# Turning batch 1's last x pair, q rest and x rest by transfer instead of on TensorE, with a new order of steps around tile 1's first products

## The chip, the cores and the metric

The kernel runs on one core of one Trainium2 chip. The metric is the device time of one execution in microseconds (us); lower is better. One execution is also recorded by the hardware profiler, and all views below come from that record.

## The reference

A linear attention over 8 batches, 8 heads, 576 tokens and a head size of 64 feeds a mixture of four dense two-layer experts, whose outputs are added with normalised weights:

```python
phi = lambda x: np.where(x > 0, x, np.exp(x) - 1.0) + 1.0
q_p, k_p = phi(q), phi(k)
kv  = einsum('bhsd,bhse->bhde', k_p, v);  z = k_p.sum(axis=2)
x   = einsum('bhsd,bhde->bhse', q_p, kv) / (einsum('bhsd,bhd->bhs', q_p, z) + 1e-6)
x   = x.transpose(0, 2, 1, 3).reshape(4608, 512)
p   = domain_probs / (domain_probs.sum(-1) + 1e-9)
out = sum over e of p[:, e] * (relu(x @ w1[e]) @ w2[e])      # 4 experts, 512 -> 1024 -> 512
```

## The kernel before

**Tiles and batches.** The 4608 rows are nine tiles of 512. Tiles 0 to 7 hold the first 512 tokens of one batch each; the last 64 tokens of every batch, its rest, are gathered in one more tile, `xT_left`, which is computed last but one. While TensorE multiplies tile j, the attention of batch j+1 is done beside it. `First` is batch 0, whose attention opens the kernel; `Batch` is every other one.

**Attention of one batch.** The raw k, v and q arrive in four pieces each (steps `load`, into a ring of six buffers, tag `raw`), the rests in `rl` (`load_left`). `k0` to `k3` and `q0` to `q3` compute phi on ScalarE, `km` and `qm` finish it on VectorE, `v0` to `v3` cast v on ScalarE into `vp`, `lk`, `lv`, `lq` do the same for the rests. `kv` multiplies k and v. q must be turned (features on the partitions) before the numerators `nd`, and their result x must be turned again into `xT` before the tile's products. A turn is done in one of two ways: four 128x128 products with an identity on TensorE and a copy out of PSUM on ScalarE (`pe_qT`, `pe_xT`, `pe_qTl`, `pe_xl`), or a transposing DMA issued on SyncE's queue (`dma_qT`, `dma_xT`, `dma_qTl`, and the end of `nd_left`). Batch 1 turns q on TensorE, three of its four x pairs by DMA, and pair 2 (`b1.xT2`), its q rest (`b1.qTl`) and its x rest (`b1.xl`) on TensorE. Batches 2 to 7 turn everything by DMA.

**Tile products.** Tile 0 of experts 1 to 3 and all later tiles use seven half-size products for layer 1, in blocks. Block d of expert e and tile j has the steps `p1.jed` to `p7.jed` and `c22.jed`. `p1` multiplies into PSUM bank b, and ScalarE copies b to bank e; `p2` adds into e and ScalarE takes the relu; `p6` adds into b and ScalarE copies it out (`u2`); `p5` starts e anew; `p7` adds into b and ScalarE copies it out (`u3`); `c22` (VectorE) takes the relu of e plus `u3`; `p4` adds into b, relu on ScalarE; `p3` adds into e, and VectorE takes the relu with `u2`. `p1` reads x pairs 0 and 1, `p2` reads pairs 2 and 3. The token sums `ts1.0` to `ts1.3` (GpSimd) feed p5, p6, p7 and p4; `ts1.1` needs pairs 2 and 3. Layer 2 of tile 0 is made of quarters: `y3.21` is expert 3, row group 2, quarter 1, two products of 512 columns; the last quarter is followed by an addition into `acc` (VectorE) and, for expert 3, by a store. Later tiles use the products `m` and the sums `hs` (GpSimd).

**Order.** Nothing is scheduled by a machine here. Every step has a name; a step that yields is resumed each time its name comes up again. The strings of `EARLY` in `CFG` list the names in the order in which the steps are emitted up to the start of tile 2, and positions in `CFG` sort the rest; every engine and every DMA queue runs its instructions in that order. All of `load`, `load_left` and the transposing DMAs of batches 1 and up stand in SyncE's one queue (but for a few loads of batch 1 on GpSimd's), and a DMA that waits there holds up all behind it.

The line that picks pair 2 in `batch_steps`, and the one that leaves batch 1 out in `nd_left`:

```python
put(at["xt"][i], f"b{b}.xT{i}", bt.pe_xT if i == 2 else bt.dma_xT, i)
for u in range(2) if self.b != 1 else ():
```

Of the kernel before, what the change touches and what calls it, by code (L numbers as in the profile page):

```python
# [12 lines left out]
FP16 = mybir.dt.float16  # L13
# [17 lines left out]
            v=(18.1, 19.16, 22.55, 30.55),  # L31
            k=(-5.5, 26.3, 27.5, 28.5),
# [5 lines left out]
            q=(36.4, 36.95, 40.2, 43.4),  # L38
            qd=(37.75, 39.0, 40.55, 44.7),
            lq=54.05,  # L40
            lqd=54.5,
            qt=(42.1, 45.0, 45.8, 46.25),
            nd=(46.7, 47.0, 47.05, 47.8),
            xt=(48.15, 50.45, 51.45, 54.8),
            qtl=57.23,
            nl=71.0,
            xl=95.55,
# [13 lines left out]
            lqd=38.3,  # L61
# [74 lines left out]
    ),  # L136
# [4 lines left out]
def kernel(  # L141
# [86 lines left out]
    def aps(shape, dtype, name, more=""):  # L228
        return ppm.tile(shape, dtype, tag=CFG["BANK"].get(now[0] + more, "s"), bufs=2, name=name)
# [67 lines left out]
    class Batch:  # L297
# [132 lines left out]
                    in_=self.ql[us].rearrange("p h d -> p (h d)"),  # L430
                )

        def pe_qTl(self):
            ps = aps([P, 2, P], FP16, "psum_ql")
            for a in range(2):
                nc.tensor.transpose(out=ps[:, a], in_=self.ql[:, 2 * a : 2 * a + 2], identity=identh)
            yield
            for u in range(2):
                us = slice(u * HP, (u + 1) * HP)
                nc.scalar.copy(out=self.qTl[:, :, u, us], in_=ps[:, :, us])  # L440

        def pe_xl(self):
            ps = aps([P, 2, P], FP16, "psum_xl")
            for a in range(2):
                nc.tensor.transpose(out=ps[:, a], in_=self.xl[:, a], identity=identh)
            yield
            c0 = self.b * SL
            for u in range(2):
                us = slice(u * HP, (u + 1) * HP)
                nc.scalar.copy(out=xT_left[:, 2 * u : 2 * u + 2, c0 : c0 + SL], in_=ps[:, :, us])  # L450

        def pe_qT(self, pair, eng=nc.vector):
            ps = aps([P, CM, P], FP16, "psum_qT")
            g, a = divmod(pair, 2)
# [59 lines left out]
        def nd_left(self, side_by_side=False):  # L514
            ps = aps([P, 3, 2, DE], FP32, "psum_nl")
            for a in range(2):
                for u in range(2):
                    us = slice(u * HP, (u + 1) * HP) if side_by_side else slice(0, P)
                    nc.tensor.matmul(  # L519
                        out=ps[us, a],  # L520
                        lhsT=self.qTl[:, a, u, us],
                        rhs=self.kvz[:, 2 * u + a],
                        start=side_by_side or u == 0,
                        stop=side_by_side or u == 1,
                        skip_group_check=side_by_side,
                    )
            yield
            self.xl = pa.tile([P, 2, P], FP16, tag="xsl", bufs=1, name="x_sl")
            self.norm(self.xl, ps, 2)
            yield  # L530
            for u in range(2) if self.b != 1 else ():
                us = slice(u * HP, (u + 1) * HP)
                c0 = self.b * SL
                nc.sync.dma_start_transpose(
                    out=xT_left[:, 2 * u : 2 * u + 2, c0 : c0 + SL],
                    in_=self.xl[us].rearrange("p a i -> p (a i)"),
                )

        def pe_xT(self, pair):
            ps = aps([P, CM, P], FP16, "psum_xT")  # L540
            for c in range(CM):
                nc.tensor.transpose(out=ps[:, c], in_=self.x[:, pair, c], identity=identh)
            yield
            if self.xT is None:
                self.new_xT()
            nc.scalar.copy(
                out=self.xT[:, pair],
                in_=ps.rearrange("p c i -> p (c i)"),
            )

        def dma_xT(self, pair):
            if self.xT is None:
# [410 lines left out]
    def batch_steps(bt, nxt, put, at, at_next):  # L963
# [34 lines left out]
            put(at["l" + n], f"b{b}.l{n}", bt.left_act, n)  # L998
            put(at["l" + n + "d"], f"b{b}.l{n}m", bt.left_dve, n)
        put(at["kv"], f"b{b}.kv", bt.kv)  # L1000
        put(at["lqd"] + 1, f"b{b}.next", load_left, "k", "v")
        put(at["lqd"] + 1.001, f"b{b}.nextq", load_left, "q")
        if not first:
            put(at["lqd"] + 2, f"b{b}.qTl", bt.dma_qTl)
        if first:
            put(at["qtl"], f"b{b}.qTl", bt.pe_qTl)
            for i in range(NPAIR):
                put(at["qt"][i], f"b{b}.qT{i}", bt.pe_qT, i, nc.scalar)
                for hf in range(2):
                    put(at["nd"][i], f"b{b}.nd{i}{hf}", bt.nd, i * CM + 2 * hf, 2)  # L1010
                put(at["xt"][i], f"b{b}.xT{i}", bt.pe_xT if i == 2 else bt.dma_xT, i)
            for i in range(NRAW):
                put(at["next"][i], f"b{b}.load{i}", load, len(mine) + i)
        else:
            for g in range(2):
                put(at["qT"][g], f"b{b}.qT{g}", bt.dma_qT, g)
            for i in range(6):
                put(at["nd"][i], f"b{b}.nd{i}", numerators, 3 * i, min(3, NPAIR * CM - 3 * i))
        if nxt is None or b in (1, 4):
            put(at["nl"] - 4.9 * (b == 4), f"b{b}.nl", bt.nd_left)  # L1020
        else:
            put(2 * NSLOT * E + at_next["kv"] - 1e-6, f"b{b}.nl", bt.nd_left, True)
        if first:
            put(at["xl"], f"b{b}.xl", bt.pe_xl)

    def warm(n):

# [9 lines left out]
    with tc.manual_schedule(  # L1037
# [76 lines left out]
        for j in range(0, NTILES - 1):  # L1114
            at = base + 2 * NSLOT * E * (j - 1) if j else 0.0

            def put(pos, *g, at=at):
                put_at(at + pos, *g)
# [65 lines left out]
```

## Time and profile before

| | |
|---|---|
| time, median of 3 runs | 483.89 us (483.45 to 484.4) |
| the profiled execution, its own time | 483.89 us |
| its span, first to last instruction | 482.1 us |
| TensorE (PE) busy | 476.2 us, 99% |
| VectorE (DVE) busy | 379.1 us, 79% |
| GpSimd (POOL) busy | 358.8 us, 74% |
| ScalarE (ACT) busy | 329.9 us, 68% |
| mean DMA rate | 112 GB/s, 54.06 MB |
| granted TensorE clock | 0.999 |

The 1.8 us between the span and the time lie outside the recorded instructions. In the views, `L897` is line 897 of the kernel before, `PE` is TensorE's products, `SPq` SyncE's DMA queue; a timeline row is start, duration, engine, line, operation, and how many instructions were merged. A PE row's duration is that of overlapping instructions, so the spacing of the starts tells what a group costs. A row of DMA issues ends with the us from issue to landing.

### The profile page before, as it was taken

The page shows a single profiled execution, that of the slowest core. Times are in us where ns is not written, and L with a number is a line of the kernel's source. Part 1 is how long each engine was busy: PE and PEld are TensorE (multiplying, and loading weights), DVE is VectorE, ACT ScalarE, POOL GpSimd, SP SyncE. Part 2 cuts the span into 40 slices and gives each one's busy share as a digit, 9 for nine tenths or more (in the row PEclk, how much of TensorE's full clock was granted, in tenths as well). Part 3 has the DMA queues.
Part 4 walks back from the last instruction along what each step waited for, and adds up shares of the span by engine and source line. Part 5 has one row for each costly group of instructions (what it writes and reads, how often), then busy time and mean ns, then how long its engine had stood idle before and what let it go on. Part 6 is the DMA issues. An engine that isn't in the chain of part 4 may idle for free.

```text
span 482.1 us, 12029 instructions
## 1 busy us (share of the span) xinstructions
PE 476.2 (99%) x4565; PEld 406.7 (84%) x4565; DVE 379.1 (79%) x794; ACT 329.9 (68%) x659; POOL 358.8 (74%) x343
## 2 busy tenths in 40 slices
PE   9999999999999999999999999999999999999996
PEld 3776757898889888988888888988898888888886
DVE  5868998897868796888678885988787756775677
ACT  4688969956795599649884888478954465446540
POOL 5666144788966986789777977697769877987775
PEclk9999999999999999999999999999999999999999
DMA  8999997532454154624562347323320020003002
GB/s 291 218 217 262 234 224 225 141 91 82 132 158 107 31 158 148 135 57 116 171 151 51 104 130 182 68 68 113 93 44 13 1 88 1 1 2 88 2 1 87
DMA packets 80489, 54.06 MB, mean 112 GB/s; under 512 B 45536, under 2 KB 73184, under 8 KB 80432
## 3 DMA queue, kind: packets, MB, share of 16 engines
q1 hardware_dynamic: 70288, 40.89, 31.9%
q0 software_dynamic: 8896, 11.34, 12.1%
q10 hardware_dynamic: 1248, 1.08, 0.7%
q8 instruction: 35, 0.57, 0.5%
q14 instruction: 22, 0.18, 0.1%
HBM read 45.16 MB, written 9.44 MB: 113 GB/s over the span
## 4 chain that ended last, share of the span: by engine, by line
PE 93%; DMA 2%; POOL 2%; DVE 1%; ACT 1%; issue 1%; SPq 0%; POOLq 0%
PE py L840 38%; PE pb L897 25%; PE pe L897 19%; PE py L745 6%; PE ph L685 1%; PE psum_nd L500 1%; DMA rawq<-in_q_dram 1%; DMA xT<-x_sb 1%; PE psum_kv L472 1%; PE pb L840 1%; POOL tt L878 1%; PE pe L840 1%; POOL hs L813 0%; POOL hs L807 0%; PE psum_nl L519 0%
## 5 line engine op out<-in xcount | busy, mean ns | idle before, releaser
L736 DVE SCALAR_TENSOR_TENSOR acc<-py,p_sb,acc 128x256 f32<-128x256 f32 (+1 forms) x382 | 182.2, 488 | 44.4 <-PE py L840 39.8
L881 DVE CUSTOM_DVE_ANT_0 h<-pe,u 128x512 f16<-128x512 f32 x140 | 96.1, 688 | 43.1 <-PE pe L897 26.1
L897 PEld LDWEIGHTS <-w 128*128 128x128 f16 x1120 | 108.7, 98 | 16.3
L807 POOL TENSOR_TENSOR hs<-h 128x512 f16<-128x512 f16 x64 | 73.8, 1154 | 55.6 <-DVE h L881 54.2
L840 PEld LDWEIGHTS <-h 128*128 128x128 f16 x1024 | 99.7, 98 | 11.6
L840 PE MATMUL py<-w,h 128*128 128x256 f16 x744 | 106.6, 273 | 0.0
L908 ACT COPY u<-pb 128x512 f32<-128x512 f32 x140 | 82.7, 593 | 31.0 <-PE pb L897 28.7
L809 POOL TENSOR_TENSOR hs<-hs,h 128x512 f16<-128x512 f16 x64 | 74.2, 1160 | 24.3 <-PE py L840 21.8
L897 PEld LDWEIGHTS <-s 128*128 128x128 f16 x840 | 81.2, 98 | 11.8
L897 PE MATMUL pb<-tt,w 128*128 128x256 f16 x560 | 83.9, 273 | 0.0
L840 PEld LDWEIGHTS <-hs 128*128 128x128 f16 x768 | 74.2, 98 | 9.2 <-POOL hs L807 0.3
L813 POOL TENSOR_TENSOR hs<-h,hs 128x512 f16<-128x512 f16 x64 | 74.8, 1168 | 1.2 <-POOL h L811 0.6
L840 PE MATMUL py<-t,hs 128*128 128x256 f16 x496 | 74.3, 273 | 0.1
L811 POOL TENSOR_TENSOR h<-h 128x512 f16<-128x512 f16 x64 | 74.3, 1161 | 0.1
L930 ACT ACTIVATE h<-pe 128x512 f16<-128x512 f32 x70 | 42.1, 601 | 41.7 <-PE pe L897 41.2
L923 ACT COPY pe<-pb 128x512 f32<-128x512 f32 x70 | 40.1, 574 | 40.1 <-PE pb L897 14.8
L951 ACT ACTIVATE h<-pb 128x512 f16<-128x512 f32 x70 | 41.9, 600 | 5.4 <-PE pb L897 5.4
L897 PE MATMUL pb<-tt,s 128*128 128x256 f16 x280 | 41.9, 273 | 0.0
L897 PE MATMUL pe<-tt,s 128*128 128x256 f16 x280 | 41.9, 273 | 0.0
L897 PE MATMUL pe<-xT,s 128*128 128x256 f16 x248 | 37.1, 273 | 0.0
L897 PE MATMUL pe<-xT,w 128*128 128x256 f16 x248 | 37.1, 273 | 0.0
L897 PE MATMUL pb<-xT,w 128*128 128x256 f16 x248 | 36.9, 273 | 0.0
(134 smaller groups left out, 596.9 us busy)
## 6 DMA issues: line engine op xcount, KB each, us to landing
w<-in_moe_w_dram POOLq DMA_DIRECT2D x14, 512.0 KB, 10.3
out_dram<-acc SPq DMA_DIRECT2D x28, 256.0 KB, 2.5
rawb<-in_k_dram SPq DMA_DIRECT2D x24, 256.0 KB, 3.2
rawb<-in_q_dram SPq DMA_DIRECT2D x24, 256.0 KB, 2.7
rawb<-in_v_dram SPq DMA_DIRECT2D x24, 256.0 KB, 3.0
out_dram<-acc SPq DMA_DIRECT2D x12, 128.0 KB, 2.3
w<-in_moe_w_dram POOLq DMA_DIRECT2D x4, 256.0 KB, 5.5
rawb<-in_k_dram POOLq DMA_DIRECT2D x4, 256.0 KB, 10.4
```

Of the source, the lines that this page charges most:

```text
L736: nc.vector.scalar_tensor_tensor(out=acc, in0=ps, scalar=pscal, in1=acc, op0=AO.mult, op1=AO.add)
L807: nc.gpsimd.tensor_tensor(out=hs[0], in0=a21, in1=a22, op=AO.add)
L809: nc.gpsimd.tensor_tensor(out=hs[1], in0=hs[0], in1=a11, op=AO.subtract)
L811: nc.gpsimd.tensor_tensor(out=a21, in0=a11, in1=a21, op=AO.subtract)
L813: nc.gpsimd.tensor_tensor(out=hs[3], in0=a12, in1=hs[1], op=AO.subtract)
L840: nc.tensor.matmul(out=ps, lhsT=lhsT(k), rhs=rhs[:, k], start=first and k == 0, stop=k == FH - 1, skip_group_check=True,)
L881: nc.vector._custom_dve(TENSOR_ADD_SAT, out=out, in0=ps, in1=u, s0=BIG, s1=0.0)
L897: nc.tensor.matmul(out=ps[:, kk], lhsT=lk(kc), rhs=rhs[:, kc], start=first and kk == 0 and kc == 0, stop=kc == 1, skip_group_check=True,)
L908: nc.scalar.copy(u, self.b)
L923: nc.scalar.copy(self.e5, self.b)
L930: nc.scalar.activation(self.h[:, :, 0, 0:NH], self.e5, AF.Relu)
L951: nc.scalar.activation(self.h[:, :, 1, 0:NH], self.b, AF.Relu)
```

## The change

The three turns of batch 1 that TensorE did go by transposing DMA; `pe_qTl`, `pe_xl` and `pe_xT` go. One step `next` that loaded the rests of k and v becomes `nextk` and `nextv`. The steps between batch 1's numerators and the first `m` products of tile 1 stand in a new order; from `b2.qm0` on the names follow as before.

```diff
-            for u in range(2) if self.b != 1 else ():
+            for u in range(2):
                 us = slice(u * HP, (u + 1) * HP)
                 c0 = self.b * SL
                 nc.sync.dma_start_transpose(
                     out=xT_left[:, 2 * u : 2 * u + 2, c0 : c0 + SL],
...
-        put(at["lqd"] + 1, f"b{b}.next", load_left, "k", "v")
-        put(at["lqd"] + 1.001, f"b{b}.nextq", load_left, "q")
-        if not first:
-            put(at["lqd"] + 2, f"b{b}.qTl", bt.dma_qTl)
+        for n in range(3):
+            put(at["lqd"] + 1 + n / 1000, f"b{b}.next" + "kvq"[n], load_left, "kvq"[n])
+        put(at["qtl"] if first else at["lqd"] + 2, f"b{b}.qTl", bt.dma_qTl)
         if first:
-            put(at["qtl"], f"b{b}.qTl", bt.pe_qTl)
...
-                put(at["xt"][i], f"b{b}.xT{i}", bt.pe_xT if i == 2 else bt.dma_xT, i)
+                put(at["xt"][i], f"b{b}.xT{i}", bt.dma_xT, i)
...
-        if first:
-            put(at["xl"], f"b{b}.xl", bt.pe_xl)
```

The order, from the third x pair on, before:

```
... b1.xT3 b1.next
b2.load2 b2.load1 b1.load4 b1.load3 b1.load2 y2.03 b1.qT2 p4.031 y2.20 y2.21 b1.qT2 b1.lq p4.030 b2.k1 y2.22 b1.load5 b1.nextq b2.load0 y2.03 b1.lqm
p3.031 b1.nd21 y2.23 y2.30 b1.nd20 y2.31 y2.32 t1.3 y2.23 b1.nd20 b1.nd21 y2.33 y2.10 b1.xT2 y2.11 y2.12 y2.13 y2.33 p3.030 y3.20 p3.031 b2.km1 p1.101
p1.100 y3.21 y3.22 y3.23 y3.30 b1.xT2 b2.k0 b2.lk p1.101 p1.100 p2.101 ts1.0 ts1.1 ts1.2 b2.ones ts1.3 b2.load4 y3.31 p6.100 p2.101 p6.100 p2.100
p2.100 b2.v3 y3.32 y3.33 p7.100 p5.101 p5.100 p7.100 b2.k2 p6.101 y3.00 y3.01 p4.100 p6.101 b2.k3 p4.100 b2.lv y3.02 p7.101 y2.13 b2.km0 t2.0 t2.1
...
```

And after:

```
... b1.xT3 b1.nextk
y2.03 b1.qT2 p4.031 y2.20 y2.21 b1.qT2 b1.lq p4.030 b2.k1 y2.22 y2.03 b1.lqm p3.031 b1.nd21 y2.23 y2.30 p3.030 b1.nd21 y2.23 y2.31 b1.nd20 y2.32
b1.nd20 y2.33 y2.10 b1.xT2 b2.load2 b2.load1 b1.load4 b1.load3 b1.load2 b1.load5 b1.nextv b1.nextq b2.load0 y2.11 y2.12 y2.33 b2.k0 y3.20 y2.13 p3.031
t1.3 ts1.0 y3.21 ts1.1 p1.100 y3.22 p1.100 ts1.2 p1.101 y3.23 p2.100 ts1.3 b2.load4 p1.101 b2.lk p2.101 p6.100 y3.30 p6.101 p2.100 p6.100 p5.100
p7.100 b2.km0 y2.13 p6.101 b2.v0 p7.100 pr1 y3.23 y3.00 y3.01 b2.km1 t3.0 t2.0 y3.02 p7.101 p4.100 b1.qTl b2.load3 b2.k2 p7.101 p2.101 p4.100 b2.v3
b2.load5 y3.23 b2.load10 b2.lv b2.v2 b2.k3 c22.100 p3.100 y3.31 ...
```

`b1.load2` fetches batch 2's v0, `b2.load2` its q0, `b2.load1` its v3, `b1.load4` v1, `b1.load3` k2 and `b1.load5` k3. `b1.nl`, which ended with the TensorE turn `b1.xl`, now ends with two transposing DMAs; they come up after the last name of `EARLY`, ahead of batch 3's four q loads.

More of the change, by code (lines that the diff above doesn't have):

```diff
@@ L431, in dma_qTl @@
                 )
[L433 to L450, printed above, removed]
         def pe_qT(self, pair, eng=nc.vector):
@@ L537, in nd_left @@
                 )
[L539 to L549, printed above, removed]
         def dma_xT(self, pair):
```

34 rows, old and new, of the table nl are left out of this document.

## Prediction

> **What bounds the kernel now.** I read the page first, then who waits for whom on PE, then PE's timeline at the three places the change touches.
>
> ```profile
> PE 476.2 (99%) x4565; PEld 406.7 (84%) x4565; DVE 379.1 (79%) x794; ACT 329.9 (68%) x659; POOL 358.8 (74%) x343
> PE warm_ps L1030 <- DVE qz L194: 1.2, 1, 1.2
> PE psum_num L658 <- DVE kvz L647: 0.6, 1, 0.6
> PE psum_num L658 <- ACT kvz L647: 0.4, 1, 0.4
> ```
>
> TensorE is busy all the time, and its three listed waits belong to the opening of batch 0 (warm-up products and `x_norm`). From there on the time is the sum of TensorE's products. Work taken from TensorE is worth its own length, work taken from others nothing, unless something new comes too late for TensorE. So the prediction has two terms: what TensorE saves, and which hand-overs become late in the new order.
>
> **What TensorE saves.** A group's cost is the spacing of starts in the timeline, since the durations overlap.
>
> ```profile
> 64.33 1.89 PE L745 MATMUL py<-w,h 128*128 128x512 f16 x8
> 66.06 0.39 PE L542 MATMUL psum_xT<-identh,x_sb 128*128 128x128 f16 x4
> 66.28 1.89 PE L745 MATMUL py<-w,h 128*128 128x512 f16 x8
> L445 PE MATMUL psum_xl<-identh,x_sl 128*128 128x128 f16 x2 | 0.3, 220 | 0.0
> 123.43 0.60 PE L897 MATMUL pb<-tt,w 128*128 128x256 f16 x4
> 123.86 0.84 PE L840 MATMUL py<-t,hs 128*128 128x256 f16 x4
> 124.54 0.60 PE L897 MATMUL pb<-tt,s 128*128 128x256 f16 x4
> ```
>
> The four products of `b1.xT2` take 66.28 - 66.06 = 0.22 us, 0.055 each. `b1.xl` has two of the same form (the L445 row), `b1.qTl` two more: eight in all, 8 x 0.055 = 0.44 us. That is the whole certain gain. One other hole is near: the group at 123.86 takes 0.68 us where its neighbour takes 0.43, so TensorE stands 0.25 us. The change touches nothing that I can tie to it, so I keep it; if it went, the gain would be 0.69. ScalarE's five copies go too, worth nothing by themselves.
>
> **Where the new order is tight: `b1.xT2`.** From 66.06 both programs have done the same on TensorE. From the rows above a quarter of layer 2 (two products of 512 columns) costs 1.73 / 4 = 0.43 us, four products of 256 columns also 0.43; I use 0.435 for a step. In the new order nine steps (y2.11, y2.12, y3.20, y2.13, y3.21, p1.100, y3.22, p1.101, y3.23) lie before p2.100, the first reader of pair 2: it is wanted at 66.06 + 9 x 0.435 = 69.97.
>
> ```profile
> 65.47 0.42 DVE L488 TENSOR_TENSOR x_sb<-psum_nd,recip 128x256 f16<-128x256 f32 x1
> 65.34 1.27 SPq L318 DMA_DIRECT2D rl<-in_v_dram  x2
> xT<-x_sb SPq DMA_TRANSPOSE x27, 2.4
> xT<-x_sb SPq DMA_TRANSPOSE x1, 5.3
> xT<-x_sb SPq DMA_TRANSPOSE x1, 8.1
> q0 software_dynamic: 818, 0.81, 122.5%
> 66.00:67.00 1.00, 1.00 (x10) 0.58 (x8) 1.00 (x2) 0.52 (x2) 0.82 (x1) 1.00 0.59 131
> 68.66 1.15 POOL L878 TENSOR_TENSOR tt<-xT 128x512 f16<-128x512 f16 x1
> ```
>
> Pair 2 is whole on VectorE at 65.47 + 0.42 = 65.9 now. In the new order one relu (p3.030) goes ahead of it and one weight difference (t1.3) goes behind it; I take these as equal. SyncE's queue is free from 65.34, because the two loads of v's rest that started there move behind. So the transfer is issued at 65.9. The median of 27 landed 2.4 us after issue: 68.3, which leaves 1.65 us. Two earlier ones of this stage took 8.1 and 5.3, while GpSimd's weight loads kept the DMA engines full (the software queue's row is from 56 to 60). By 66 that queue is empty and the DMA share is 0.59 (last but one row), so I take 2.4, and keep 8.1 as the far end. The Trainium skill, "DMA: Bandwidth & Descriptors", section "Queues, rings and completion order", has each DMA engine alternate between the queues that have work for it, packet by packet. By that rule 2.4 holds here and 8.1 doesn't, since no software transfer is moved; the trace agrees as far as the shares go. GpSimd's sums behind the transfer, 1.15 each, would be ready at 69.5 (ts1.1; p6.100 wants it at 70.85) and 70.6 (ts1.2; p7.100 wants it at 72.59). No loss here.
>
> **Where it is late: batch 2's v0.** The transfer stands in SyncE's queue ahead of six raw loads, and it waits there for VectorE; they wait with it.
>
> ```profile
> 66.71 0.55 SPq L340 DMA_DIRECT2D rawb<-in_q_dram  x1
> 68.89 0.42 SPq L340 DMA_DIRECT2D rawb<-in_v_dram  x1
> 132.35 2.45 SPq L534 DMA_TRANSPOSE xT_left<-x_sl  x2
> rawb<-in_q_dram SPq DMA_DIRECT2D x1, 256.0 KB, 3.0
> rawb<-in_v_dram SPq DMA_DIRECT2D x1, 256.0 KB, 4.4
> rawb<-in_k_dram SPq DMA_DIRECT2D x1, 256.0 KB, 5.6
> ```
>
> A transposing DMA holds the queue 2.45 / 2 = 1.2 us, so the first raw load goes out at 65.9 + 1.2 + 0.1 = 67.2 instead of 66.71, and v0, the fifth, at 68.89 + 0.5 = 69.4. It took 4.4 us to land (five 256 KB loads go out within 2.2 us and share the engines); the first of the six took 3.0, the last 5.6. I take its own 4.4: 73.8. Ends: 72.4 and 75.0.
>
> When does ScalarE want it? The old order cast v3 first, long after v0 was issued; the new one casts v0 first.
>
> ```profile
> 68.01 0.84 ACT L399 ACTIVATE kz<-rl 64x256 f16<-64x256 f32 x2
> 68.88 0.39 ACT L401 ACTIVATE psum_el<-rl 128x256 f32<-128x256 f32 x1
> 69.20 1.03 ACT L923 COPY pe<-pb 128x512 f32<-128x512 f32 x2
> 70.61 0.60 PE L897 MATMUL pe<-xT,w 128*128 128x256 f16 x4
> 71.30 0.60 ACT L930 ACTIVATE h<-pe 128x512 f16<-128x512 f32 x1 [1.07 <-PE pe L897]
> 72.11 0.59 ACT L908 COPY u<-pb 128x512 f32<-128x512 f32 x1 [0.21 <-PE pb L897]
> 72.61 0.60 ACT L930 ACTIVATE h<-pe 128x512 f16<-128x512 f32 x1
> 78.16 1.69 ACT L381 CAST vp<-rawb 128x512 f16<-128x512 f32 x3
> L881 DVE CUSTOM_DVE_ANT_0 h<-pe,u 128x512 f16<-128x512 f32 x140 | 96.1, 688 | 43.1 <-PE pe L897 26.1
> ```
>
> ScalarE starts 0.69 us after the group that it waits for (71.30 against 70.61). p1.101 begins on TensorE at 66.06 + 7 x 0.435 = 69.10, so its copy begins at 69.79. Behind it stand, by the spacing of these rows: the copy 0.48, the k rest 0.87, its exponential 0.32, the relu of p2.100 0.50, the copies `u2` of p6.100 and p6.101 0.50 each. ScalarE is at v0 at 72.95. It waits there 73.8 - 72.95 = 0.85 us. A cast takes (1.69 - 0.63) / 2 = 0.53, so the copy `u3` of p7.100, queued behind it, runs from 74.4 and takes 0.59: ready at 75.0.
>
> Two readers want `u3`. p4.100 overwrites what `u3` copies; it is the 21st step after 66.06, wanted at 66.06 + 20 x 0.435 = 74.76, and so comes 0.2 late. c22.100 on VectorE reads `u3`, 0.69 long: ready at 75.7; p3.100, which TensorE reaches at 75.0 + 0.435 = 75.4, waits 0.3 more for it. Together 0.5 us of standing. Before it p7.100 wants the `u2` copy of p6.100 (71.95 + 0.59 = 72.54) at 72.59, an edge that costs 0 to 0.1; I count it within the 0.5. Behind it VectorE has slack again, since TensorE is late by the same 0.5. If v0 lands at the early end, 72.4, ScalarE doesn't wait and nothing is lost; at the late end, 75.0, ScalarE waits 2.05 and TensorE stands 0.5 + 1.2 = 1.7.
>
> **Covered parts.** The rows that do it:
>
> ```profile
> 114.44 0.37 SPq L340 DMA_DIRECT2D rawb<-in_k_dram  x1
> 117.27 8.82 SPq L340 DMA_DIRECT2D rawb<-in_q_dram  x4
> 84.76 0.42 SPq L717 DMA_DIRECT2D out_dram<-acc  x1
> out_dram<-acc SPq DMA_DIRECT2D x28, 256.0 KB, 2.5
> 87.89 0.50 ACT L734 ACTIVATE acc<-py,p_sb 128x256 f32<-128x256 f32 x1
> ```
>
> The x rest's two transfers fall into SyncE's idle time between 114.44 + 0.37 = 114.8 and 117.27; they need 2.45 us and fill it. Without that cover the four q loads behind them would slip by as much, of the 8.8 us they spend waiting for buffers anyway. Nobody reads the result before the last but one tile. The q rest's two transfers hold up two q loads and four stores by 2.45 us. The store that frees the fourth `acc` buffer goes out just ahead of the last one in the new order, about 84.7 by that one's row, and lands at 84.7 + 2.5 = 87.2, before ScalarE's addition at 87.89: 0.7 us of slack, which each further us of lateness would eat and then cost ScalarE.
>
> **The sum.** The profiled execution took 483.89 us, which is the median too, so no correction is needed. 483.89 - 0.44 + 0.5 = 483.95 us.
>
> **The rivals.**
>
> *v0 in time.* Its load lands within 3.55 us (69.4 to 72.95). For it: the first load took 3.0, and the two rest loads that were ahead are gone. Against it: the transposing DMA has taken their place, and v0 has four raw loads ahead. Only the gain is left: 483.89 - 0.44 = 483.45; with the hole at 123.86 gone too, 483.2. Chance 0.22.
>
> *v0 very late.* It lands like k3, 5.6 us after issue: 483.89 - 0.44 + 1.7 = 485.15. Slower. It decides from a landing about 5.2 us after issue. Chance 0.14.
>
> *Pair 2 late.* The transfer lands more than 69.97 - 65.9 = 4.1 us after issue; from then every us is a us of TensorE, while v0's wait melts away behind it. At 5.3 us: 483.89 - 0.44 + 1.2 = 484.65; at 8.1: 483.89 - 0.44 + 4.0 = 487.45. It is slower by what can be told from 5.5 us on. Against it stands the empty software queue. Chance 0.08.
>
> *Turns dearer than they look.* If a turn held TensorE for more than its spacing, eight of them would bring more. The starts give no room: 66.28 follows 66.06 by 0.22 and the next products run at full pace, so at the 220 ns that the L445 row gives for one instruction it would be 8 x 0.22 = 1.8 us, 482.1 without other losses. The Trainium skill, "TensorE: Matmul & The Clock Gate", section "Part 4: PE-mode transpose", gives about 275 ns for one such turn within a kernel, which would make it 2.2 us, an estimate from that page; the trace's 55 ns contradicts it as a cost. Chance 0.05.
>
> **How the numbers follow.** About 0.2% (1 us) is what a measurement of this kernel can tell from no change. My forecast, 483.95, has 0.51, with 483.6 to 484.4 around it. Within 0.2% (482.9 to 484.9) lie the forecast, v0 in time, and a little of the late cases: 0.51 + 0.22 + 0.04 = 0.77. Slower by more: most of v0 very late (0.13) and most of pair 2 late (0.05): 0.18. Faster by more: only dearer turns, 0.05. The range from 483.2 to 485.0 leaves out the far part of the two late cases and the dear turns.
>
> **What would show it.** In the profile after: no rows of the identity products outside batch 0 and `b1.qT`; an xT transfer issued near 65.9 and landing near 68.3; v0's load issued near 69.4; ScalarE idle before its first cast, released by a DMA, near 73; and PE starts with a hole of 0.2 to 0.5 us near 75, before the groups of p4.100 and p3.100. A PE without holes from 66 to 90 makes v0 in time the right case; a hole just before p2.100 makes pair 2 the culprit; holes after 90 that were not there before would mean that I missed a hand-over.

## The result and the profile after

| | before | after |
|---|---|---|
| median of 6 runs | 483.86 us (483.35 to 484.47) | 486.12 us (485.81 to 487.49) |
| profiled execution | 483.89 us | 485.82 us |
| its span | 482.1 us | 484.0 us |
| granted TensorE clock | 0.999 | 1.000 |

The ratio is 1.0049, 95% interval 1.0034 to 1.0063: slower by some 2.3 us, outside the predicted range (483.2 to 485.0), where no difference was the likeliest. In the kernel after, other line numbers stand for the same code: L866 is the products `p`, L714 tile 0's layer 2, L809 the products `m`, L877 the copies `u2` and `u3`, L703 ScalarE's addition into `acc`, L686 the store, L523 the transfer of an x pair.

The first part of the page (busy us, share, instructions):

```profile
PE 476.6 (98%) x4557; PEld 406.1 (84%) x4557; DVE 379.1 (78%) x794; ACT 329.0 (68%) x654; POOL 359.0 (74%) x343
```

Who waits for whom on PE (us in total, times, the longest):

```profile
PE py L809 <- ACT acc L703: 0.9, 2, 0.5
PE pb L866 <- ACT u L877: 0.6, 1, 0.6
```

TensorE has eight products fewer, as meant, and two kinds of waits that the kernel before didn't list. The first place is the predicted one. ScalarE's timeline of the kernel after (start, us, engine, line, and in brackets the idle time before with its releaser):

```profile
71.92 1.07 ACT L877 COPY u<-pb 128x512 f32<-128x512 f32 x2
74.35 0.62 ACT L381 CAST vp<-rawb 128x512 f16<-128x512 f32 x1 [1.36 <-DMA rawb<-in_v_dram]
74.88 0.58 ACT L877 COPY u<-pb 128x512 f32<-128x512 f32 x1
```

PE's timeline there:

```profile
74.30 0.60 PE L866 MATMUL pb<-tt,w 128*128 128x256 f16 x4
75.51 0.61 PE L866 MATMUL pb<-tt,w 128*128 128x256 f16 x4 [0.62 <-ACT u L877]
76.23 0.60 PE L866 MATMUL pe<-xT,s 128*128 128x256 f16 x4
```

SyncE's queue in the timeline:

```profile
65.86 1.24 SPq L523 DMA_TRANSPOSE xT<-x_sb  x1
67.14 0.58 SPq L340 DMA_DIRECT2D rawb<-in_q_dram  x1
67.83 0.90 SPq L340 DMA_DIRECT2D rawb<-in_v_dram  x2
68.83 0.43 SPq L340 DMA_DIRECT2D rawb<-in_k_dram  x1
69.35 0.42 SPq L340 DMA_DIRECT2D rawb<-in_v_dram  x1
```

The DMA issues of narrow windows, with us from issue to landing (pair 2's transfer, v0):

```profile
xT<-x_sb SPq DMA_TRANSPOSE x1, 3.0
rawb<-in_v_dram SPq DMA_DIRECT2D x1, 256.0 KB, 4.8
```

v0's load went out at 69.35 and landed 4.8 later. ScalarE stood 1.36 us before its cast, the copy `u3` behind it began at 74.88, and TensorE stood before p4.100 and p3.100: 75.51 - 74.30 - 0.435 = 0.77 and 76.23 - 75.51 - 0.435 = 0.28.

The second place wasn't in the sum. ScalarE's timeline of the kernel after:

```profile
89.84 0.47 ACT L703 ACTIVATE acc<-py,p_sb 128x256 f32<-128x256 f32 x1 [0.94 <-DMA out_dram<-acc]
```

SyncE's queue:

```profile
85.02 0.37 SPq L340 DMA_DIRECT2D rawb<-in_v_dram  x1
85.48 0.89 SPq L686 DMA_DIRECT2D out_dram<-acc  x2
```

PE's timeline:

```profile
89.78 1.19 PE L809 MATMUL py<-w,hs 128*128 128x256 f16 x8
90.80 0.60 PE L866 MATMUL pe<-xT,s 128*128 128x256 f16 x4
91.77 0.60 PE L809 MATMUL py<-w,h 128*128 128x256 f16 x4 [0.37 <-ACT acc L703]
```

The landing of the store issued at 85.48:

```profile
out_dram<-acc SPq DMA_DIRECT2D x1, 256.0 KB, 4.3
```

What SyncE's queue waited for from 78 to 87 us (us in total, times, the longest):

```profile
SPq L340 <- ACT psum_ee L371: 2.1, 3, 1.4
```

ScalarE needs an `acc` buffer at 89.84 - 0.94 = 88.90; the store that frees it went out at 85.48, right behind a load of batch 3, and landed at 89.8. That load (85.02) had itself stood in the queue, 1.4 us, for a raw buffer that ScalarE had still to read. TensorE stood 91.77 - 90.80 - 0.435 = 0.53, and 0.15 (1.02 less eight products' 0.87) just before. The third place is late, PE's timeline again:

```profile
242.49 0.60 PE L866 MATMUL pb<-xT,w 128*128 128x256 f16 x4
243.58 0.60 PE L809 MATMUL py<-w,h 128*128 128x256 f16 x4 [0.49 <-ACT acc L703]
```

That is 0.65 us. The hole of 0.25 that the kernel before had at 123.86 isn't there. With three short holes near 72.6, 78.0 and 92.5, 0.18 together, the account closes: -0.44 - 0.25 + 1.05 + 0.68 + 0.65 + 0.18 = +1.87, against 485.82 - 483.89 = 1.93 in the profiled executions.

### The profile page after: what moved, and what is told of

Same layout as the page of the kernel before. It is cut to its first block, busy times and chain, and to the rows that moved or that the text cites. A ratio compares the mean times of both kernels' runs of the same rounds, so it can differ in the third digit from the quotient of the medians.

```text
span 484.0 us, 12015 instructions
## 1 busy us (share of the span) xinstructions
PE 476.6 (98%) x4557; PEld 406.1 (84%) x4557; DVE 379.1 (78%) x794; ACT 329.0 (68%) x654; POOL 359.0 (74%) x343
## 4 chain that ended last, share of the span: by engine, by line
PE 91%; DVE 3%; DMA 3%; ACT 1%; issue 0%; SPq 0%; ACTq 0%; DVEq 0%
PE py L809 38%; PE pb L866 24%; PE pe L866 18%; PE py L714 4%; PE ph L654 1%; PE psum_nd L481 1%; DMA rawq<-in_q_dram 1%; DMA rawb<-in_v_dram 1%; DMA out_dram<-acc 1%; PE psum_kv L453 1%; PE pb L809 1%; DVE h L850 1%; PE pe L809 1%; DVE acc L705 0%; PE psum_nl L500 0%; DVE kpos L565 0%
## 5 line engine op out<-in xcount | busy, mean ns | idle before, releaser
L866 PEld LDWEIGHTS <-w 128*128 128x128 f16 x1120 | 108.7, 98 | 17.8 <-ACT u L877 1.1
L809 PEld LDWEIGHTS <-h 128*128 128x128 f16 x1024 | 99.7, 98 | 12.9 <-issue 1.2
L809 PE MATMUL py<-w,h 128*128 128x256 f16 x744 | 106.4, 273 | 0.9 <-ACT acc L703 0.9
L877 ACT COPY u<-pb 128x512 f32<-128x512 f32 x140 | 82.6, 592 | 29.9 <-PE pb L866 27.7
L866 PEld LDWEIGHTS <-s 128*128 128x128 f16 x840 | 81.1, 98 | 11.9 <-issue 0.3
L866 PE MATMUL pb<-tt,w 128*128 128x256 f16 x560 | 83.9, 273 | 0.6 <-ACT u L877 0.6
L809 PEld LDWEIGHTS <-hs 128*128 128x128 f16 x768 | 74.2, 98 | 8.9 <-issue 0.3
L809 PE MATMUL py<-t,hs 128*128 128x256 f16 x496 | 74.1, 273 | 0.0
L866 PE MATMUL pe<-tt,s 128*128 128x256 f16 x280 | 42.0, 273 | 0.0
L866 PE MATMUL pb<-tt,s 128*128 128x256 f16 x280 | 41.9, 273 | 0.0
L866 PE MATMUL pe<-xT,s 128*128 128x256 f16 x248 | 37.1, 273 | 0.1
L866 PE MATMUL pb<-xT,w 128*128 128x256 f16 x248 | 37.1, 273 | 0.0
L809 PE MATMUL py<-w,hs 128*128 128x256 f16 x248 | 37.0, 273 | 0.0
```

The costliest lines, as they stand in the source:

```text
L809: nc.tensor.matmul(out=ps, lhsT=lhsT(k), rhs=rhs[:, k], start=first and k == 0, stop=k == FH - 1, skip_group_check=True,)
L866: nc.tensor.matmul(out=ps[:, kk], lhsT=lk(kc), rhs=rhs[:, kc], start=first and kk == 0 and kc == 0, stop=kc == 1, skip_group_check=True,)
L877: nc.scalar.copy(u, self.b)
```

## The experiments

All ratios are to the kernel before, in five rounds on the same chip for the kernels of one job; the kernel before had medians of 484.01 (E1 to E4), 483.65 (E5 to E8) and 484.12 us (E10 to E13; the numbers go by the runs' names). The opening of batch 0 differs by up to about 0.6 us between executions of any of these kernels, so differences below that are read from the holes, not from one execution's time.

| | edit | median, us | ratio, 95% interval |
|---|---|---|---|
| E1 | after, v0's load first of the six | 484.77 | 1.0013 (1.0004 to 1.0023) |
| E2 | after, the store ahead of batch 3's loads | 485.17 | 1.0031 (1.0019 to 1.0043) |
| E3 | both | 483.71 | 1.0002 (0.9993 to 1.0010) |
| E4 | old order, turns by transfer | 484.21 | 1.0002 (0.9993 to 1.0011) |
| E5 | new order, turns on TensorE | 485.12 | 1.0037 (1.0024 to 1.0050) |
| E6 | before, one turn eight times | 485.00 | 1.0026 (1.0016 to 1.0035) |
| E7 | after, two later loads moved by position | 485.52 | 1.0041 (1.0027 to 1.0056) |
| E8 | E3, the same move | 483.77 | 1.0004 (0.9995 to 1.0012) |
| E10 | after, pair 2 alone on TensorE | 484.60 | 1.0011 (1.0001 to 1.0021) |
| E11 | E3, the two loads behind `qT0` | 483.85 | 0.9993 (0.9981 to 1.0005) |
| E12 | before, the two loads behind `qT0` | 484.28 | 1.0006 (0.9997 to 1.0015) |
| E13 | E4, the two loads behind `qT0` | 484.01 | 1.0001 (0.9988 to 1.0013) |

**E1: v0's load first.** Theory: the place of v0's load in SyncE's queue makes the first holes.

```diff
-b1.xT2 b2.load2 b2.load1 b1.load4 b1.load3 b1.load2 b1.load5
+b1.xT2 b1.load2 b2.load1 b1.load4 b1.load3 b2.load2 b1.load5
```

> The changed kernel with one edit: in SyncE's queue the load of batch 2's v0 takes the place of q0's, first of the six instead of fifth. Theory (late v0): the holes near 74.3 and 75.5 us (0.77 and 0.28) go, since v0 would land near 71 and ScalarE wants it at 73.0; the hole near 91 stays, because the store of y3.0 still stands behind the batch 3 loads: 486.1 - 1.05 = 485.1 us. Rival (the transfers themselves crowd queue and DMA engines, whatever is loaded first): some other load or the turn becomes late, 486 us.

ScalarE's timeline of E1:

```profile
72.58 0.65 ACT L381 CAST vp<-rawb 128x512 f16<-128x512 f32 x1
...
89.03 0.47 ACT L703 ACTIVATE acc<-py,p_sb 128x256 f32<-128x256 f32 x1 [1.12 <-DMA out_dram<-acc]
```

Who waits on PE:

```profile
PE py L809 <- ACT acc L703: 1.2, 3, 0.6
PE psum_kv L453 <- ACT vp L381: 0.2, 1, 0.2
```

The cast waits for nothing and the holes at 74 to 76 are gone. A new one of 0.40 stands at 80.3: the products `kv` wait for a later piece of v, whose load ScalarE awaited for 0.54 us up to 78.08. The store's wait stays and its holes grow (0.34 and 0.53, against 0.15 and 0.53), though TensorE is now only 0.40 late ahead of it instead of 1.05. So the second place has a cause of its own.

**E2: the store ahead of the loads.**

```diff
-p4.101 y3.33 b2.load7 ... b3.load1 y3.03 p1.111
+p4.101 y3.33 y3.03 b2.load7 ... b3.load1 p1.111
```

> The changed kernel with one edit: the store of y3.0 is issued right behind that of y3.3, ahead of three loads for batch 3, as in the kernel before. Theory (late store): ScalarE's wait of 0.94 us at 89.8 and the holes near 89.8 and 90.8 (0.14 and 0.53) go, those at 74 to 76 stay: 486.1 - 0.6 = 485.5 us. Rival (the second hole is only the echo of the first): no change, 486.1 us.

SyncE's queue in the timeline of E2:

```profile
81.86 1.08 SPq L686 DMA_DIRECT2D out_dram<-acc  x2
...
85.31 0.37 SPq L340 DMA_DIRECT2D rawb<-in_v_dram  x1
```

Who waits on PE:

```profile
PE pb L866 <- ACT u L877: 0.7, 1, 0.7
```

The store leaves by 82.9 instead of 85.48, so its data had been ready: it was the loads ahead of it, the last of which goes out only at 85.31, that held it. The holes at 89.8 and 90.8 are gone, those at 74 to 76 stay.

**E3: both.**

> Both edits. Theory: all holes from 66 to 95 us go, 486.1 - 1.05 - 0.65 = 484.4 us; if the hole of 0.65 near 242 us was an accident of one execution and not of the change, its profile need not show it and the time is 483.5 to 484. Rival (echo): as the first edit alone, 485.1 us.

No hole over 0.1 us is left between 66 and 95, and the time is that of before. Both causes together account for the loss, as far as the medians tell (483.71 against 484.01). Holes of 0.15, 0.64 and 0.36 remain at 138, 190 and 241.

**E4: the turns without the new order.** The kernel before, with its three turns by transfer; so that the queue can run, the six raw loads and the rests of v and q stand behind `b1.xT2`.

```diff
-put(at["xt"][i], f"b{b}.xT{i}", bt.pe_xT if i == 2 else bt.dma_xT, i)
+put(at["xt"][i], f"b{b}.xT{i}", bt.dma_xT, i)
...
-... y2.10 b1.xT2 y2.11 ...
+... y2.10 b1.xT2 b2.load2 b2.load1 b1.load4 b1.load3 b1.load2 b1.load5 b1.nextv b1.nextq b2.load0 y2.11 ...
```

> The kernel before with the three turns by transfer and only SyncE's queue changed for it: the six raw loads and the rests of v and q stand behind b1.xT2, every engine keeps its old order (v3 is cast first, v0 five us later). Theory: the turn is not what costs; the eight products leave TensorE, 483.86 - 0.44 = 483.4 us, up to 483.9 if k3's load comes late for ScalarE. Rival (crowding): slower than before by a us or more, with holes behind p2.101 or near 76.

SyncE's queue in the timeline of E4:

```profile
69.00 0.42 SPq L340 DMA_DIRECT2D rawb<-in_v_dram  x1
```

ScalarE's timeline:

```profile
77.54 1.69 ACT L381 CAST vp<-rawb 128x512 f16<-128x512 f32 x3
```

v0's load goes out at 69.00, nearly as late as after the change, and nothing waits: the old order casts v0 only at 77.54. No hole until 138. By 95 us, the opening left out, the trace has saved 0.33 over before (0.22 for pair 2, 0.11 for the q rest), and the hole at 123.86 is gone; one of 0.14 at 138 takes part of it back. In the time the saving can't be told from nothing.

**E5: the order without the turns.** The kernel after with `pe_xT`, `pe_qTl` and `pe_xl` put back.

> The changed kernel's order with the three turns back on TensorE (the copy of pair 2 out of PSUM stands ahead of b2.k0, the q rest's ahead of b2.load3, b1.xl where it was before). Theory, the order of SyncE's queue: with no transposing DMA ahead of the six raw loads they go out as soon as their buffers are free, so v0 is in time and the holes at 74 to 76 go; the last store of tile 0 still stands behind batch 3's loads, so the holes near 89 to 91 stay as in the run with v0 first (0.34 + 0.53); eight identity products come back (0.44): 484.77 + 0.44 = 485.2. Rival, the new order of ScalarE's and VectorE's work is by itself too tight near 74: holes of 0.5 or more stay there, 485.9 or more. Rival, the turns by transfer are to blame as such (their traffic, their landing): without them no hole between 66 and 95, 484.0.

ScalarE's timeline of E5:

```profile
73.08 0.65 ACT L381 CAST vp<-rawb 128x512 f16<-128x512 f32 x1
...
75.70 0.43 ACT L440 COPY qz<-psum_ql 128x128 f16<-128x128 f16 x2 [1.49 <-PE psum_ql L436]
```

Who waits on PE:

```profile
PE pb L897 <- ACT h L951: 1.3, 1, 1.3
```

v0 is cast without a wait, so it is the transfer ahead of it that made it late. But the run says nothing of the rest: the q rest's copies, which I had put ahead of `b2.k2`, held ScalarE 1.49 us and made a hole of their own, 1.45 by the spacing of the starts, and with TensorE that late nobody waited for the store. The time came out as the theory said, for another reason.

**E10: pair 2 alone back on TensorE**, which E5 had left unsaid.

```diff
-put(at["xt"][i], f"b{b}.xT{i}", bt.dma_xT, i)
+put(at["xt"][i], f"b{b}.xT{i}", bt.pe_xT if i == 2 else bt.dma_xT, i)
...
-y2.33 b2.k0 y3.20
+y2.33 b1.xT2 b2.k0 y3.20
```

> The changed kernel with pair 2 of x alone turned on TensorE again (its copy out of PSUM ahead of b2.k0); q rest and x rest stay with the transfers, the loads' order stays. Theory: it is the transfer standing ahead of the raw loads that made v0 late; without it they go out as early as 65.3 to 66, v0 lands by 72 and ScalarE casts it without waiting; the holes at 74 to 76 go, those at 90 stay (0.34 + 0.53, as with v0 first), four identity products come back (0.22): 484.77 + 0.22 = 485.0. Rival, the new order is too tight at 74 even with v0 in time, or the copy that comes back onto ScalarE is what is late there: holes there of 0.5 or more, 485.7.

SyncE's queue in the timeline of E10:

```profile
68.45 0.42 SPq L340 DMA_DIRECT2D rawb<-in_v_dram  x1
```

ScalarE's timeline:

```profile
73.14 0.65 ACT L381 CAST vp<-rawb 128x512 f16<-128x512 f32 x1
...
89.62 0.47 ACT L715 ACTIVATE acc<-py,p_sb 128x256 f32<-128x256 f32 x1 [1.09 <-DMA out_dram<-acc]
```

Without the transfer v0's load is 0.90 earlier and the cast doesn't wait. The holes of 0.77 and 0.28 go, those of the store's wait stay near 90 and 91 (0.30 and 0.53). The rival that the returning copy is late has a small part: 0.22 before 75.92, of which the waits put 0.2 down to `u3`, now behind one copy more on ScalarE; and TensorE stood 0.25 before 73.53, for which the trace names no releaser. By the ratios, 1.0049 and 1.0011, the transfer of pair 2 in this place cost 0.0038 of the time, 1.8 us, to save 0.22; the two intervals leave some 1.0 to 2.7. The holes account for less: 1.05 went, 0.22 + 0.25 came, and four products came back. The profiled execution of E10 was the slowest of its twelve, 485.81, no faster than that of the kernel after; its late holes sum to 1.25, against 0.65. So E10 shows what made v0 late, while the price of 1.8 us isn't traced in full.

**E6: the price of a turn.** `pe_xT` does its four products eight times over.

```diff
-            for c in range(CM):
+            for c in list(range(CM)) * 8:
```

> The kernel before with the four identity products of b1.xT2 repeated eight times, 28 more. It measures a turn's price. Theory: 0.055 us each as the starts in the timeline are spaced, 28 x 0.055 = 1.54: 485.55. Rival, the price that the Trainium skill gives ('TensorE: Matmul & The Clock Gate', 'Part 4: PE-mode transpose', about 275 ns): 28 x 0.275 = 7.7: 491.7. Rival, hidden behind other work: 484.0.

PE's timeline of E6:

```profile
65.52 1.95 PE L542 MATMUL psum_xT<-identh,x_sb 128*128 128x128 f16 x32
67.31 1.89 PE L745 MATMUL py<-w,h 128*128 128x512 f16 x8
```

32 products take 67.31 - 65.52 = 1.79 us, 0.056 each. The time rose by 485.00 - 483.65 = 1.35 us for 28 more, 0.048 each (0.03 to 0.06 by the interval). The 275 ns that the Trainium skill gives ("TensorE: Matmul & The Clock Gate", "Part 4: PE-mode transpose") would have been 7.7 us, an estimate from that page; the measurement decides for the spacing of the starts.

**E7 and E8: the late holes, first try.** Theory: two loads that follow a tile's last two stores slow them down. The edit adds 3 to their positions.

```diff
-(2.8 if (n, i) == ("q", 0) else 1)
+(2.8 if (n, i) == ("q", 0) else 1) + 3 * (m in (8, 9))
```

> The changed kernel with the two loads of the next batch that go out right behind a tile's last two stores (load8 and load9 of batches 3 and on) three steps later, about 2.7 us. Theory for the hole at 242 (0.65; in other kernels with the new order 0.15 to 0.8 at 140, 190 and 242): the two 256 KB loads share the DMA engines with the two stores, which then land 4.4 instead of 3.2 us after issue, and ScalarE's first addition of the next tile waits for the buffer; with the loads later the stores land within 3.5 and these holes go, while those at 74 to 76 and 90 stay: 486.1 - 0.65 = 485.4. Rival, the stores are late because of the lateness handed on from the first holes, or by chance: holes after 130 stay, 486.1.

> The changed kernel with v0's load first, the last store of tile 0 ahead of batch 3's loads, and load8 and load9 of batches 3 and on three steps later. Theory: the holes at 138, 190 and 241 that the kernel with the first two kept (0.15 + 0.64 + 0.36 = 1.15) go: 483.7 - 1.1 = 482.6, faster than before. Rival, they don't depend on these loads: 483.7.

SyncE's queue in the timeline of E7:

```profile
239.18 0.82 SPq L686 DMA_DIRECT2D out_dram<-acc  x2
240.09 0.40 SPq L340 DMA_DIRECT2D rawb<-in_v_dram  x1
240.58 1.51 SPq L340 DMA_DIRECT2D rawb<-in_k_dram  x1
```

The loads still went out right behind the stores: between the old position and the new one SyncE has nothing to wait for, and a position only sorts a queue. So these two say nothing of the theory and are repeats: E7 of the kernel after (ratio 1.0041 beside 1.0049; holes of 0.93 and 0.28 at 74 to 76, 0.53 at 90.9, 0.57 at 191, 0.18 at 243), E8 of E3.

**E11 to E13: the late holes, second try.** The two loads stand behind the transfer of q, which waits for VectorE.

```diff
-put(at[n][i] + (2.8 if (n, i) == ("q", 0) else 1), f"b{b}.load{m}", load, m + NRAW)
+put(at["qT"][0] + m / 1000 if m in (8, 9) else at[n][i] + (2.8 if (n, i) == ("q", 0) else 1), f"b{b}.load{m}", load, m + NRAW)
```

> The kernel with v0's load first and the store ahead, and load8 and load9 of batches 3 and on put behind the transfer of the first half of q (b.qT0), which waits for VectorE until about 140: in the queue they stand behind a real wait, some 4 us after the stores. (Three steps later by position, as tried before, left them right behind the stores, since SyncE had nothing to wait for between.) Theory: the stores then land in 3.5 us or less and the holes at 138, 190 and 241 go: 483.75 - 0.6 to 1.1 = 482.7 to 483.1. Rival, the stores' landing doesn't hang on these loads: 483.75, holes there as before.

> Control: the kernel before, with load8 and load9 of batches 3 and on behind b.qT0. It had no holes at 138, 190 and 241 in its profile: 483.7 to 484.0, no difference. Rival, executions of it that aren't profiled have such holes too, and the edit takes them away: 483.3 or less.

> The kernel before with the three turns by transfer in the old order of the engines (raw loads behind b1.xT2), and load8 and load9 of batches 3 and on behind b.qT0. Theory: its turns saved 0.33 by 95 us and its holes at 138 and later cost 0.29; without those holes it is 0.4 to 0.7 below before: 483.0 to 483.3. Rival, the holes stay: 483.6 to 483.9.

SyncE's queue in the timeline of E11:

```profile
186.23 0.81 SPq L686 DMA_DIRECT2D out_dram<-acc  x2
191.79 1.23 SPq L420 DMA_TRANSPOSE qT<-qp  x1
193.08 0.57 SPq L340 DMA_DIRECT2D rawb<-in_v_dram  x1
```

The landing of those two stores:

```profile
out_dram<-acc SPq DMA_DIRECT2D x2, 256.0 KB, 4.3
```

Who waits on PE in E11:

```profile
PE py L809 <- ACT acc L703: 0.7, 3, 0.3
```

PE's timeline of E12:

```profile
291.87 0.60 PE L897 MATMUL pb<-xT,w 128*128 128x256 f16 x4
292.84 0.60 PE L840 MATMUL py<-w,h 128*128 128x256 f16 x4 [0.37 <-ACT acc L734]
```

Now nothing follows the stores for 4.7 us, and they still take 4.3; holes of 0.35, 0.43 and 0.38 remain in E11. My theory of the late holes falls. In all fourteen traces the late holes stand just where the first store of such a pair took 3.9 to 4.6 us to land, and nowhere where it took up to 3.8: it is this landing that ScalarE, and behind it TensorE, waits for. E12, the kernel before with this edit alone, has two such holes (0.53 at 291.9, 0.16 at 343), so the old order isn't free of them. Between 130 and 345 us they sum to 0.6 to 1.25 in eight profiled executions with the new order (none in E5, where those stores landed in 2.6 to 3.7), and to 0, 0, 0.14, 0.32 and 0.69 in the five with the old one. That points to the new order having more of them, and would account for E3 being no faster than before though its early holes are gone; but one execution of each can't show it, and why the stores land late there stays open. None of E11 to E13 can be told from the kernel before, so no version here is faster than it. (The 0.29 in E13's text counts a hole of 0.16 near 468, which every trace has, that of before too.)

## Why the prediction was wrong

**TensorE's saving: right.** E6 gives 0.048 to 0.056 us for a product where the sum had 0.055; E4 shows the 0.33 of pair 2 and the q rest in the trace. The rival of dearer turns falls.

**Pair 2: right.** Its transfer went out at 65.86 (65.9 predicted), landed in 3.0 us instead of 2.4, before its reader; TensorE stood nowhere ahead of p2.100.

**v0: the mechanism right, the size wrong.** ScalarE was there at 74.35 - 1.36 = 72.99 (72.95 predicted), the load went out at 69.35 (69.4). The mis-sized term is the landing: 4.8 us, not the 4.4 of the row of before. With some 0.2 from landing to cast, `u3` was ready 0.45 later than predicted, and as predicted for later landings all of that fell on TensorE: 1.05 us of holes instead of 0.5. It came out between the forecast and the rival *v0 very late*, 1.1 to that rival's 1.7. E1 and E10 show the cause: with v0's load ahead of the others, or without the transfer ahead of it, the holes go. Why the load took 4.8 us isn't shown.

**The store: the step that failed.** I set it down as covered, by the median landing of 28 stores, 2.5 us. The stores of this very stretch, in the trace of before, each in its own narrow window:

```profile
out_dram<-acc SPq DMA_DIRECT2D x1, 256.0 KB, 3.3
out_dram<-acc SPq DMA_DIRECT2D x1, 256.0 KB, 4.7
out_dram<-acc SPq DMA_DIRECT2D x1, 256.0 KB, 3.9
```

They are the ones issued at 75.95, 79.81 and 84.76. With the 4.3 that it measured, 84.7 + 4.3 = 89.0 is 1.1 us behind the 87.89 at which ScalarE wants the buffer, and E1, where v0 is in time, shows just that: a wait of 1.12 us, 0.34 + 0.53 of holes. I had put the price on record as what each us of lateness would cost, but no rival carried it; the sign of a missed hand-over that I named, new holes after 90, did come. This mistake alone, at E1's 0.87, moves the forecast to 484.8, and v0's second half to 485.4. With the holes as the profiled execution has them, 483.95 + 0.55 (v0) + 0.68 (store) + 0.65 (at 242) + 0.18 (the short ones) - 0.25 (at 123.86) = 485.76; it took 485.82. In E2 the same data leave by 82.9, so its place behind batch 3's loads, not the addition before it, is what held the store.

**The late hole at 242 (0.65) and the lost hole at 123.86 (0.25): not in the sum.** The first belongs to the late holes, which E12 has in the old order too and whose cause is open. The second is absent in E3 and E4, whose x rest goes by transfer, and there in E12, whose x rest TensorE turns (0.31 at 123.6); but E5 and E6, where TensorE came later, lack it as well, so its mechanism stays open.

**The covered transfers: right.** No wait in any trace goes back to the transfers of the x rest or the q rest.

## What to carry to other kernels

In SyncE's queue an instruction that waited for an engine made everything behind it late: pair 2's transfer held v0's load, and a load that waited for its buffer held the store. So moving a 0.2 us piece of work to a transfer is worth what the loads and stores queued behind it can bear: list each with its issue, landing and reader, and put the one wanted first at the front. Take the landing of a transfer from its neighbours in time, not from the median over the whole kernel, and if that leaves less slack than the spread of those neighbours, give it a rival. Changing a step's position delays nothing by itself: in a queue only a real wait between two entries separates them.

## What the runs showed of the hardware

A 128x128 product with the identity, in a train of 32, costs TensorE 0.056 us, though each row lasts 219 ns.

Of two 256 KB stores issued back to back with no load behind them for over 4 us, the first landed in 4.1 to 4.2 us (E11, near 135, 186 and 238); with two loads right behind them it took 3.9 to 4.4 (E3, at the same three places). So the loads behind aren't what slows them here. What does is open; in the kernel before the same pairs of stores landed in 2.6 to 3.9.

The issue of one raw load holds SyncE's queue for 0.4 us in most rows and for 1.0 to 2.3 in up to four of a trace's 72 (240.58 in E7, 1.51), without a change in the program around it.
